# Bank ring left to the fill products, w_out scaled off GpSimd, ones of v written once, and new engine lists

## Chip, cores and metric

One core of one Trainium2 chip runs the whole program. The metric is the device time of one execution in microseconds; the kernel before takes 240.79 us (median of 3 runs, 240.64 to 241.34). Engines: TensorE (PE; PEld is its weight load), VectorE (DVE), ScalarE (ACT), GpSimd (POOL) and SyncE (SP), whose queue issues nearly all transfers.

## What is computed

```python
# q, k, v: (8 batches, 8 heads, 576 rows, 64); p: (8, 8, 32, 64); all float32
def sm_attn(qq, kk, vv):                       # softmax attention, scale 1/8
    s = scale * np.matmul(qq, kk.transpose(0, 1, 3, 2))
    a = np.exp(s - np.max(s, axis=-1, keepdims=True))
    a = a / (np.sum(a, axis=-1, keepdims=True) + 1e-09)
    return np.matmul(a, vv)
p_packed = sm_attn(p, k, v)                    # 32 packed rows per head
out = sm_attn(q, p_packed, p_packed)
x = out.transpose(0, 2, 1, 3).reshape(4608, 512)
h = x @ w_in                                   # 512 x 2048
g = h * (1.0 / (1.0 + np.exp(-beta * h)))
return g @ w_out                               # 2048 x 512, float32
```

## The kernel before

Eight batches of 576 rows go through three stages that overlap: attention over the packed rows, the first layer (`h`, then `g` on ScalarE), the second layer (`o` or `p`/`P` products into the output). The second softmax is folded into the first layer: `W = pp x w_in`, scaled by `beta` (L944), replaces x @ w_in, and `A2` holds the normalised weights. `w_out` is divided by `beta` row by row when it is cast to bf16 (`cast_out`, L1466).

- The order of work is written out by hand. `SEQUENCE` (L86) holds one list of task keys for each of PE, ACT, DVE, POOL and SP. A planner (`Planner.run`, L305) walks the lists with a cost for each task and emits the instructions; on the chip each engine runs its list in order, and an instruction that waits holds up everything behind it on its engine.
- A task key names its kind and batch: `("h", b, ft)` is one 128-column block of the first layer (two matmuls of 512 columns, 0.43 us), `("g", b, ft)` its activation; `("o", 0, t, ft)` one pair of second-layer matmuls of batch 0; `("p"/"P", b, i, ...)` the seven half-size products that stand for eight in batches 1 to 7, which need sums of `w_out` quarters (`("T4", i)`, L1133, all sixteen `w_out` blocks first) and sums of `g` (`("S", b, i)`); `("w", b, n)` and `("W", b, m)` the fused weights on PE and their scaling on DVE; `("s1", b, i)`, `("pun", b)`, `("s2", b, i)`, `("z2", b, i)` the attention products; `("hr", b, half)` the remaining 64 rows of a batch; `("take"/"add", 0, t)` reads of an output bank.
- Batches 0 and 1 are transposed on PE (`tr`, `trr`), batches 2 to 7 by transfers (`("tr", b, "k" or "q", 0)` on SP, L597). Each input has one float32 buffer, so the load of batch b waits for the casts of batch b - 1; the casts of batches 2 to 7 all run on POOL (`piece`, L506; `tail`, L520). For v, `piece` also writes the column of ones that counts the softmax sum (L511), once in each batch.
- The weights come through three staging buffers: `ld_in` 0, 1, `ld_out` 0, 1, `ld_in` 2, 3, `ld_out` 2, the rest of p, `ld_out` 3. Each waits for the casts of the load three places before it (`put_in` and `put_out`, L1471 and L1476). A `w_in` load is cast in two tasks `("w_in", n, i)`, a `w_out` load in four `("w_out", 4n + i)`.
- PSUM has eight banks in three rings: "h" (2), "o" (2), "att" (4). `HOME` (L63) puts single attention tasks of the start into a ring other than their own. Where a list leaves PE idle by the planner's costs in the first 60 us, `fill` (L344) lets `keep_warm` (L440) emit 128-column products on `ones`, but only while a bank of ring "o" is free; these products go into that bank.

Of the kernel before, what the change touches and what calls it, by code (L numbers as in the profile page):

```python
# [48 lines left out]
PE_BATCHES = 2  # L49
def TILED(key):  # L50
# [19 lines left out]
    ("s1", 0, 1): "h",  # L70
    ("z1", 0): "o",
    ("s2", 0, 1): "h",
    ("z2", 0, 0): "o",
    ("z2", 0, 1): "o",
    ("z2", 0, 2): "o",
# [1476 lines left out]
```

## Time and profile before

| | us |
|---|---|
| median of 3 runs | 240.79 |
| the profiled execution | 241.07 |
| its span, first to last instruction | 239.3 |
| PE busy in the span | 224.5 (94%) |
| ACT busy | 171.3 (72%) |
| DVE busy | 160.9 (67%) |
| POOL busy | 82.5 (34%) |
| mean granted TensorE clock | 0.986 of full speed |
| transfers, queue of SP | 53.75 MB, 81.5% of 16 engines' span |

The profiled execution lies 1.8 us above its span (start and end of the program) and 0.3 us above the median. PE has the largest share of busy time, but the share is a mean over a start that waits for data and a long stretch without gaps, so the stages are looked at one by one.

### The profile page before, as it was taken

The page shows a single profiled execution, that of the slowest core. Times are in us where ns is not written, and L with a number is a line of the kernel's source. Part 1 is how long each engine was busy: PE and PEld are TensorE (multiplying, and loading weights), DVE is VectorE, ACT ScalarE, POOL GpSimd, SP SyncE. Part 2 cuts the span into 40 slices and gives each one's busy share as a digit, 9 for nine tenths or more (in the row PEclk, how much of TensorE's full clock was granted, in tenths as well). Part 3 has the DMA queues.
Part 4 walks back from the last instruction along what each step waited for, and adds up shares of the span by engine and source line. Part 5 has one row for each costly group of instructions (what it writes and reads, how often), then busy time and mean ns, then how long its engine had stood idle before and what let it go on. Part 6 is the DMA issues. An engine that isn't in the chain of part 4 may idle for free.

```text
span 239.3 us, 6112 instructions
## 1 busy us (share of the span) xinstructions
PE 224.5 (94%) x2550; PEld 152.9 (64%) x2576; DVE 160.9 (67%) x254; ACT 171.3 (72%) x312; POOL 82.5 (34%) x90
## 2 busy tenths in 40 slices
PE   7887899986999999999999999999999999999993
PEld 6554353333477765775588567876786578677883
DVE  4569647884897945986798855852788279515751
ACT  3619679874899977977679678896788679665300
POOL 3223448398873160624151730540354000000000
PEclk9999589999999999999999999999999999999999
DMA  6999999999999999999999899969794040022044
GB/s 216 396 387 399 401 350 348 290 325 224 263 263 191 274 275 245 218 320 242 230 279 331 225 236 303 225 128 221 160 313 147 3 175 3 1 86 92 0 122 144
DMA packets 67107, 54.14 MB, mean 226 GB/s; under 512 B 38948, under 2 KB 58532, under 8 KB 66568
## 3 DMA queue, kind: packets, MB, share of 16 engines
q1 hardware_dynamic: 67072, 53.75, 81.5%
q8 instruction: 20, 0.33, 0.6%
q14 instruction: 7, 0.06, 0.1%
q10 hardware_dynamic: 8, 0.01, 0.0%
HBM read 37.23 MB, written 9.44 MB: 195 GB/s over the span
## 4 chain that ended last, share of the span: by engine, by line
PE 72%; DMA 11%; POOL 5%; ACT 4%; DVE 3%; issue 2%; SPq 1%; POOLq 0%; DVEq 0%
PE o_ps L421 42%; PE h_ps L421 19%; DMA k<-in_k_dram 6%; DMA w_in<-in_moe_w_in_dram 5%; POOL w_out_bf L1469 3%; PE w_ps L421 3%; PE hr_ps L421 3%; PE s_ps L421 2%; PE pp_ps L421 1%; PE z_ps L421 1%; ACT g_main L992 1%; POOL k_bf L515 1%; DVE g_main L1223 1%; DVE W_bf L957 1%; ACT L438 1%
## 5 line engine op out<-in xcount | busy, mean ns | idle before, releaser
L992 ACT ACTIVATE g_main<-h_ps 128x512 bf16<-128x512 f32 x128 | 72.2, 596 | 34.9 <-PE h_ps L421 28.1
L421 PEld LDWEIGHTS <-g_main 128*128 128x128 bf16 x624 | 58.8, 98 | 25.8 <-issue 5.3
L421 PE MATMUL h_ps<-A2T,W_bf 128*128 128x512 bf16 x233 | 68.5, 390 | 1.8 <-DVE A2T L890 1.0
L421 PE MATMUL o_ps<-w_out_bf,g_main 128*128 128x256 bf16 (+1 forms) x397 | 61.2, 289 | 2.3 <-POOL w_out_bf L1469 1.9
L421 PEld LDWEIGHTS <-W_bf 128*128 128x128 bf16 x512 | 33.2, 99 | 20.6 <-issue 6.6
L950 DVE TENSOR_TENSOR W_bf<-w_ps,beta_bc 128x512 bf16<-128x512 f32 x48 | 30.6, 684 | 15.8 <-PE w_ps L421 15.8
L421 PE MATMUL o_ps<-w_sum,g_sum 128*128 128x256 bf16 x256 | 33.1, 273 | 0.6 <-DVE o_sb L1253 0.4
L421 PE MATMUL o_ps<-w_sum,g_main 128*128 128x256 bf16 x224 | 31.3, 273 | 0.3
L1253 DVE TENSOR_TENSOR o_sb<-o_ps,o_sb 128x512 f32<-128x512 f32 (+1 forms) x27 | 17.0, 630 | 18.9 <-PE o_ps L421 15.6
L438 ACT ACT_TABLE_LOAD x22 | 28.2, 1283 | 1.1 <-PEq L1536 0.7
L421 PEld LDWEIGHTS <-g_sum 128*128 128x128 bf16 x256 | 24.3, 98 | 6.3 <-issue 1.0
L515 POOL CAST q_bf<-q 128x1024 bf16<-128x1024 f32 x12 | 13.6, 1151 | 31.2 <-DMA q<-in_q_dram 31.2
L515 POOL CAST v_bf<-v 128x1024 bf16<-128x1024 f32 x12 | 15.6, 1326 | 22.4 <-DMA v<-in_v_dram 22.4
L1255 ACT COPY o_sb<-o_ps 128x512 f32<-128x512 f32 (+1 forms) x16 | 8.1, 506 | 14.1 <-PE o_ps L421 14.1
L515 POOL CAST k_bf<-k 128x1024 bf16<-128x1024 f32 x12 | 13.3, 1124 | 12.8 <-DMA k<-in_k_dram 12.8
L1255 DVE COPY o_sb<-o_ps 128x512 f32<-128x512 f32 (+1 forms) x20 | 13.2, 661 | 4.1 <-PE o_ps L421 4.0
L957 DVE SCALAR_TENSOR_TENSOR W_bf<-w_ps,rz,beta_bc 128x512 bf16<-128x512 f32 x15 | 10.4, 745 | 4.2 <-PE w_ps L421 4.2
L890 DVE TENSOR_TENSOR A2T<-E2T,rz 128x512 bf16<-128x512 bf16 x16 | 11.6, 733 | 2.1 <-ACT rz L885 1.8
L1469 POOL TENSOR_SCALAR w_out_bf<-w_out,rbeta 128x512 bf16<-128x512 f32 x6 | 10.6, 1768 | 4.8 <-DMA w_out<-in_moe_w_out_dram 4.7
L1223 DVE TENSOR_TENSOR g_sum<-g_main 128x2048 bf16<-128x2048 bf16 x7 | 9.0, 1283 | 3.9 <-ACT g_main L992 3.9
L421 PE MATMUL w_ps<-w_in_bf,pp 64*32 64x512 bf16 x252 | 11.1, 389 | 0.0
L873 ACT ACTIVATE rz<-z_ps 128x512 f32<-128x512 f32 x16 | 9.6, 604 | 1.9 <-PE z_ps L421 1.9
(131 smaller groups left out, 281.3 us busy)
## 6 DMA issues: line engine op xcount, KB each, us to landing
k<-in_k_dram SPq DMA_DIRECT2D x6, 1024.0 KB, 8.7
v<-in_v_dram SPq DMA_DIRECT2D x6, 1024.0 KB, 8.3
q<-in_q_dram SPq DMA_DIRECT2D x6, 1024.0 KB, 9.2
out_dram<-o_sb SPq DMA_DIRECT2D x10, 512.0 KB, 3.7
w_in<-in_moe_w_in_dram SPq DMA_DIRECT2D x4, 1024.0 KB, 11.5
w_out<-in_moe_w_out_dram SPq DMA_DIRECT2D x4, 1024.0 KB, 10.7
out_dram<-o_sb SPq DMA_DIRECT2D x12, 256.0 KB, 3.8
k<-in_k_dram SPq DMA_DIRECT2D x4, 576.0 KB, 6.4
```

The lines of the kernel that those rows point to most:

```text
L421: return self.nc.tensor.matmul(out, lhsT, rhs, start=start, stop=stop, tile_position=pos, skip_group_check=True)
L438: self.nc.scalar.preload_act_table_set(SETS[mode])
L515: self.copy[engine](o[:, 0 : 32 * e].rearrange("p (t h e) -> p h t e", t=4, h=8)[:, h, :, 0:D], t[:, 0:2048].rearrange("p (h t d) -> p h t ...
L873: nc.scalar.activation(st[b, "rz2"][:, i], ps[:], AF.Ln)
L890: nc.vector.tensor_tensor(part(st[b, "A2"], i), part(st[b, "E2"], i), st[b, "rz2"][:, i] if i < 2 else st[b, "rz2r"][:], ALU.mult)
L950: nc.vector.tensor_tensor(st[b, "W"][:, r, cols].rearrange("q (f p) -> q f p", f=4), st[b, "w", m][:].rearrange("q (p f) -> q f p", f=4), ...
L957: nc.vector.scalar_tensor_tensor(st[b, "W"][:, r, cols].rearrange("q (f p) -> q f p", f=4), st[b, "w", m][:].rearrange("q (p f) -> q f p", ...
L992: nc.scalar.activation(st[b, "g"][:, ft, :], st[b, "h", ft][:], AF.Silu)
L1223: nc.vector.tensor_tensor(o, x, y, op)
L1253: nc.vector.tensor_tensor(o, x, o, ALU.add)
L1255: self.copy[engine](o, x)
L1469: nc.scalar.mul(o, w, r) if engine == "ACT" else {"DVE": nc.vector, "POOL": nc.gpsimd}[engine].tensor_scalar_mul(o, w, r)
```

## The change

Four things are changed.

1. `HOME`: no attention task of the start goes into ring "o" any more; `p0_tr`, `trr 0 k`, `s1r 0`, `z2 0 2`, `w 0 0`, `tr 1 k 0` go to "h", `bcol` and `brow` 0 to 3 to "att", `tr 1 q 0` stays in "att". Ring "o" is then free until the first second-layer product.
2. `cast_out` has no GpSimd form: POOL's six `w_out` blocks (4, 6, 8, 10, 12, 15) go to DVE, but for 12, which goes to ACT (ACT gives 7 and 14 to DVE and takes 1). DVE scales 13 of the 16 blocks, before 7.
3. The ones of v are written once, in the first batch cast by `piece`; the later batches use the same tile.
4. All five lists are in a new order. On DVE, `w_in` blocks (1, 0), before, become (1, 1), (2, 0), (3, 0), and `p_bf` comes from POOL. POOL takes casts of batches 0 and 1 from ACT. SP loads k of batch 0 ahead of p0, v of batch 1 ahead of `ld_out` 0, k of batch 2 ahead of `ld_in` 3, and q of batch 2 ahead of `ld_out` 3 and of v of batch 2.

```diff
 HOME = {
-    ("brow", 0): "o",
-    ("brow", 2): "o",
+    ("p0_tr",): "h",
+    ("bcol",): "att",
+    ("brow", 0): "att",
...
-    ("s1r", 0): "o",
+    ("s1r", 0): "h",
...
-    ("w", 0, 0): "o",
-    ("tr", 1, "k", 0): "o",
+    ("z2", 0, 2): "h",
+    ("w", 0, 0): "h",
+    ("tr", 1, "k", 0): "h",
...
-    ("tr", 1, "q", 0): "o",
...
     "PE": [
-        ("z2", 0, 0), ("brow", 3), ("s2", 0, 1), ("z2", 0, 1), ("s1r", 1), ("s1", 1, 1), ("w", 0, 0), ("s1", 1, 0),
-        ("z2", 0, 2), ("h", 0, 1), ("h", 0, 0), ("w", 0, 1), ("z1", 1), ("h", 0, 2), ("h", 0, 3), ("tr", 1, "q", 0),
...
+        ("z2", 0, 0), ("tr", 1, "k", 1), ("trr", 1, "k"), ("z2", 0, 1), ("s2", 0, 1), ("s1r", 1), ("s1", 1, 0),
+        ("w", 0, 0), ("s1", 1, 1), ("w", 0, 1), ("z2", 0, 2), ("z1", 1), ("h", 0, 3), ("h", 0, 1), ("pun", 1, 0),
+        ("pun", 1), ("h", 0, 0), ("h", 0, 2), ("tr", 1, "q", 0), ("h", 0, 5), ("h", 0, 4), ("tr", 1, "q", 1),
+        ("h", 0, 6), ("h", 0, 7), ("w", 1, 0), ("o", 0, 0, 1), ("o", 0, 2, 1), ("o", 0, 2, 3), ("trr", 1, "q"),
+        ("s2", 1, 0), ("o", 0, 0, 3), ("o", 0, 0, 5), ("o", 0, 2, 5), ("z2", 1, 0), ("o", 0, 0, 7), ("o", 0, 2, 7),
+        ("z2", 1, 1), ("w", 0, 2), ("w", 1, 1), ("s2", 1, 1), ("o", 0, 3, 1), ("o", 0, 3, 3), ("w", 1, 2),
...
+        ("o", 0, 0, 13), ("h", 1, 14), ("h", 1, 8), ("o", 0, 2, 9), ("h", 1, 12), ("o", 0, 2, 11), ("s1r", 2),
+        ("hr", 0, 0), ("h", 1, 15), ("o", 0, 0, 15), ("o", 0, 2, 13), ("s1", 2, 1), ("s1", 2, 0), ("o", 0, 2, 15),
+        ("o", 0, 3, 9), ("o", 0, 3, 11), ("hr", 0, 1), ("o", 0, 3, 13), ("o", 0, 3, 15), ("p", 1, 1, 0),
...
     "DVE": [
...
-        ("i1", 0), ("px", 0), ("T", 1, "k", 0), ("pn", 0), ("beta", 2), ("T", 1, "k", 1), ("rk", 1), ("w_in", 0, 1),
-        ("A2", 0, 0), ("w_in", 1, 0), ("W", 0, 0), ("W", 0, 1), ("A2", 0, 1), ("W", 0, 2), ("W", 0, 3), ("w_out", 0),
-        ("w_out", 1), ("i1", 1), ("w_out", 2), ("T", 1, "q", 0), ("T", 1, "q", 1), ("pp", 1), ("px", 1), ("w_out", 5),
...
+        ("pp", 0), ("rq", 0), ("px", 0), ("T", 1, "k", 0), ("beta", 3), ("T", 1, "k", 1), ("w_in", 0, 1), ("rk", 1),
+        ("A2", 0, 0), ("W", 0, 0), ("w_in", 1, 1), ("W", 0, 1), ("A2", 0, 1), ("W", 0, 2), ("W", 0, 3),
+        ("cast", 1, "q", 0), ("pp", 1), ("i1", 1), ("T", 1, "q", 0), ("px", 1), ("w_out", 0), ("w_out", 2),
+        ("T", 1, "q", 1), ("W", 1, 0), ("w_out", 5), ("w_out", 4), ("w_out", 6), ("w_out", 7), ("W", 1, 1),
+        ("w_in", 2, 0), ("rq", 1), ("take", 0, 0), ("W", 0, 4), ("W", 0, 5), ("take", 0, 2), ("W", 1, 2),
+        ("A2", 0, 2), ("W", 1, 3), ("A2", 1, 0), ("A2", 1, 1), ("W", 1, 4), ("w_in", 3, 0), ("W", 1, 5), ("p_bf",),
+        ("W", 0, 6), ("W", 0, 7), ("take", 0, 3), ("w_out", 9), ("w_out", 8), ("w_out", 11), ("take", 0, 1),
+        ("W", 1, 6), ("w_out", 10), ("W", 1, 7), ("pT1", 0, 1), ("pT1", 1, 0), ("w_out", 13), ("w_out", 14),
+        ("w_out", 15), ("T4", 1), ("add", 0, 1), ("T4", 2), ("T4", 3), ("T4", 4), ("add", 0, 0), ("S", 1, 1),
...
     "POOL": [
-        ("cast", 1, "q", 0), ("cast", 1, "q", 1), ("cast", 1, "v", 1), ("w_out", 4), ("pn", 1), ("w_out", 6),
-        ("w_in", 2, 1), ("w_in", 3, 1), ("w_in", 3, 0), ("cast", 2, "k", 0), ("w_out", 8), ("cast", 2, "k", 1),
-        ("cast", 2, "k", 2), ("p_bf",), ("w_out", 10), ("w_out", 15), ("w_out", 12), ("cast", 2, "v", 0),
...
+        ("w_in", 0, 0), ("pn", 0), ("w_in", 1, 0), ("cast", 1, "v", 0), ("cast", 1, "v", 1), ("cast", 1, "q", 1),
+        ("pn", 1), ("cast", 2, "k", 0), ("cast", 2, "k", 1), ("w_in", 3, 1), ("cast", 2, "k", 2), ("cast", 2, "q", 0),
...
     "SP": [
...
+        ("ld", 0, "v", 1), ("ld", 1, "k", 0), ("ld", 1, "k", 1), ("ld_in", 0), ("ld_in", 1), ("ld", 1, "v", 0),
+        ("ld", 1, "v", 1), ("ld", 1, "q", 0), ("ld", 1, "q", 1), ("ld_out", 0), ("ld_out", 1), ("ld_in", 2),
+        ("ld", 2, "k", 0), ("ld_in", 3), ("ld", 2, "k", 2), ("ld", "p"), ("ld_out", 2), ("ld", 2, "q", 0),
+        ("ld_out", 3), ("ld", 2, "q", 2), ("tr", 2, "k", 0), ("ld", 2, "v", 0), ("ld", 2, "v", 2), ("ld", 3, "k", 0),
...
-                if i == 0:
+                if i == 0 and x == "v" and b > PE_BATCHES:
+                    self.t[b, x] = self.t[b - 1, x]
+                elif i == 0:
...
-            nc.scalar.mul(o, w, r) if engine == "ACT" else {"DVE": nc.vector, "POOL": nc.gpsimd}[engine].tensor_scalar_mul(o, w, r)
+            nc.vector.tensor_scalar_mul(o, w, r) if engine == "DVE" else nc.scalar.mul(o, w, r)
```

## Rows read from the trace of the kernel before

**Rows 1.** Page, busy tenths, granted clock and transfers in 40 slices of 5.98 us.

```profile
PE   7887899986999999999999999999999999999993
PEclk9999589999999999999999999999999999999999
DMA  6999999999999999999999899969794040022044
```

**Rows 2.** Stages: us, PE PEld DVE ACT POOL busy (count), clock, transfer share, GB/s.

```profile
25.00:30.00 5.00, 4.79 (x33) 2.13 (x33) 2.88 (x6) 3.29 (x6) 2.30 (x2) 0.50 1.06 403
30.00:35.00 5.00, 4.95 (x67) 2.96 (x66) 1.92 (x5) 3.64 (x6) 2.44 (x2) 0.86 0.93 347
80.00:100.00 20.00, 19.72 (x239) 13.02 (x240) 14.00 (x19) 16.06 (x31) 8.85 (x10) 1.00 1.11 252
```

**Rows 3.** PE in order of time: start, us, work [idle before <-releaser], to 57 us.

```profile
23.96 0.23 PE L421 MATMUL z2r_ps<-E2T,bones 128*128 128x128 bf16 x1 [1.18 <-DVE W_bf L957]
25.21 1.44 PE L421 MATMUL h_ps<-A2T,W_bf 128*128 128x512 bf16 x3 [1.02 <-DVE A2T L890]
...
56.94 0.59 PE L421 MATMUL o_ps<-w_out_bf,g_main 128*128 128x512 bf16 x2 [1.90 <-POOL w_out_bf L1469]
57.37 0.59 PE L421 MATMUL h_ps<-A2T,W_bf 128*128 128x512 bf16 x2
```

**Rows 4.** DVE in order of time: a cast, a pair of neighbours, the last T4.

```profile
22.55 0.69 DVE L1458 CAST w_in_bf<-w_in 128x1024 bf16<-128x1024 f32 x1 [0.47 <-DMA w_in<-in_moe_w_in_dram]
...
39.22 0.68 DVE L1054 COPY o_sb<-o_ps 128x512 f32<-128x512 f32 x1
39.82 1.41 DVE L957 SCALAR_TENSOR_TENSOR W_bf<-w_ps,rz,beta_bc 128x512 bf16<-128x512 f32 x2
...
64.39 1.38 DVE L1133 TENSOR_TENSOR w_sum<-w_out_bf,w_sum 128x2048 bf16<-128x2048 bf16 x1
```

**Rows 5.** Weight tiles: durations in ns min/median/max, and issue to landing.

```profile
L1469 DVE TENSOR_SCALAR w_out_bf<-w_out,rbeta x7: 471/656/925, 28.6 to 51.2; 128x512 bf16<-128x512 f32 x7
L1469 POOL TENSOR_SCALAR w_out_bf<-w_out,rbeta x6: 1557/1567/2625, 33.7 to 55.3; 128x512 bf16<-128x512 f32 x6
DMA to landing us min/median/max: 8.7/10.7/15.1
...
L1458 DVE CAST w_in_bf<-w_in x2: 694/1016/1337, 20.1 to 22.6; 128x1024 bf16<-128x1024 f32 x2
```

**Rows 6.** DVE groups from 36 to 66 us: count | busy, mean ns.

```profile
L957 DVE SCALAR_TENSOR_TENSOR W_bf<-w_ps,rz,beta_bc 128x512 bf16<-128x512 f32 x12 | 8.3, 745 | 2.1 <-PE w_ps L421 2.1
L1133 DVE TENSOR_TENSOR w_sum<-w_out_bf 128x2048 bf16<-128x2048 bf16 x2 | 3.3, 1639 | 0.6 <-POOL w_out_bf L1469 0.6
L1133 DVE TENSOR_TENSOR w_sum<-w_out_bf,w_sum 128x2048 bf16<-128x2048 bf16 x2 | 2.8, 1376 | 0.0
```

**Rows 7.** POOL in order of time: weights, ones, v of batch 3.

```profile
33.71 1.57 POOL L1469 TENSOR_SCALAR w_out_bf<-w_out,rbeta 128x512 bf16<-128x512 f32 x1 [1.38 <-DMA w_out<-in_moe_w_out_dram]
...
51.02 5.87 POOL L1469 TENSOR_SCALAR w_out_bf<-w_out,rbeta 128x512 bf16<-128x512 f32 x3
56.84 0.25 POOL L511 MEMSET v_bf<- 128x36 bf16 x1
...
83.13 2.02 POOL L515 CAST v_bf<-v 128x1024 bf16<-128x1024 f32 x2 [8.23 <-DMA v<-in_v_dram]
85.10 0.46 POOL L522 CAST v_bf<-v 128x256 bf16<-128x256 f32 x1
```

**Rows 8.** SP's queue in order of time: `ld_out` 3.

```profile
41.17 0.35 SPq L1462 DMA_DIRECT2D w_out<-in_moe_w_out_dram  x1
```

**Rows 9.** PE in order of time: first product of batch 1, pun of batch 3.

```profile
66.75 0.63 PE L421 MATMUL hr_ps<-A2T,W_bf 128*128 128x64 bf16 x16
67.22 0.60 PE L421 MATMUL o_ps<-w_out_bf,g_main 128*128 128x256 bf16 x4
...
87.33 0.49 PE L421 MATMUL pp_ps<-v_bf,E1T 128*32 128x65 bf16 x40
```

More of the change, by code (lines that the diff above doesn't have):

```diff
@@ L63 @@
 HOME = {
-    ("brow", 0): "o",
-    ("brow", 2): "o",
+    ("p0_tr",): "h",
+    ("bcol",): "att",
+    ("brow", 0): "att",
+    ("brow", 1): "att",
+    ("brow", 2): "att",
     ("brow", 3): "att",
+    ("trr", 0, "k"): "h",
     ("tr", 0, "q", 1): "h",
-    ("s1r", 0): "o",
+    ("s1r", 0): "h",
     ("s1", 0, 0): "h",
[L70 to L75, printed above, removed]
-    ("w", 0, 0): "o",
-    ("tr", 1, "k", 0): "o",
+    ("z2", 0, 2): "h",
+    ("w", 0, 0): "h",
+    ("tr", 1, "k", 0): "h",
     ("tr", 1, "k", 1): "h",
-    ("tr", 1, "q", 0): "o",
     ("s1", 1, 1): "h",
     ("s2", 1, 0): "h",
+    ("s2", 1, 1): "h",
     ("z2", 1, 0): "h",
@@ L87 @@
     "PE": [
[75 rows of a table removed]
[75 rows of a table added]
     ],
     "ACT": [
[37 rows of a table removed]
[36 rows of a table added]
     ],
     "DVE": [
[7 rows of a table removed]
-        ("W", 1, 6), ("W", 1, 7), ("w_out", 9), ("take", 0, 3), ("w_out", 11), ("w_out", 13), ("T4", 1),
[22 rows of a table removed]
[8 rows of a table added]
+        ("W", 0, 6), ("W", 0, 7), ("take", 0, 3), ("w_out", 9), ("w_out", 8), ("w_out", 11), ("take", 0, 1),
[24 rows of a table added]
     ],
     "POOL": [
-        ("cast", 0, "q", 0), ("cast", 0, "v", 0), ("cast", 1, "k", 0), ("w_in", 0, 0), ("w_in", 1, 1),
-        ("cast", 1, "q", 0), ("cast", 1, "q", 1), ("cast", 1, "v", 1), ("w_out", 4), ("pn", 1), ("w_out", 6),
-        ("w_in", 2, 1), ("w_in", 3, 1), ("w_in", 3, 0), ("cast", 2, "k", 0), ("w_out", 8), ("cast", 2, "k", 1),
-        ("cast", 2, "k", 2), ("p_bf",), ("w_out", 10), ("w_out", 15), ("w_out", 12), ("cast", 2, "v", 0),
[1 row of a table removed]
+        ("cast", 0, "k", 1), ("cast", 0, "q", 0), ("cast", 0, "v", 0), ("cast", 1, "k", 0), ("cast", 1, "k", 1),
+        ("w_in", 0, 0), ("pn", 0), ("w_in", 1, 0), ("cast", 1, "v", 0), ("cast", 1, "v", 1), ("cast", 1, "q", 1),
[2 rows of a table added]
         ("cast", 3, "k", 0), ("cast", 3, "k", 2), ("cast", 3, "k", 1), ("cast", 3, "q", 0), ("cast", 3, "q", 1),
@@ L245 @@
         ("cast", 5, "k", 2), ("cast", 5, "v", 0), ("cast", 5, "v", 1), ("cast", 5, "v", 2), ("cast", 6, "k", 0),
[4 rows of a table removed]
[4 rows of a table added]
     ],
     "SP": [
[14 rows of a table removed]
-        ("store", 12), ("store", 11), ("store", 14), ("store", 13), ("store", 16, 0), ("store", "r1", 0),
-        ("store", "r1", 1), ("store", 17, 1), ("store", 16, 1), ("store", 17, 0),
[14 rows of a table added]
+        ("store", 11), ("store", 14), ("store", 13), ("store", "r1", 0), ("store", "r1", 1), ("store", 16, 0),
+        ("store", 17, 1), ("store", 16, 1), ("store", 17, 0),
     ],
@@ L540, in plan_loads @@
             else:
-                c0 = self.task(("cast", b, x, 0), "POOL", 0.97, lambda f=piece: f("POOL", 0, 4), [m0] + old, rank + 3)
+                c0 = self.task(("cast", b, x, 0), "POOL", 1.35 if b == PE_BATCHES and x == "v" else 0.97, lambda f=piece: f("POOL", 0, 4), [m0] + old, rank + 3)
                 self.task(("cast", b, x, 1), "POOL", 0.97, lambda f=piece: f("POOL", 1, 4), [m0, c0], rank + 3)
@@ L1479, in put_out @@
                 [
-                    self.task(("w_out", 4 * n + i), {"DVE": 0.4, "ACT": 0.7, "POOL": 0.8}, None, lambda e, i=i: cast_out(e, n, i), [ld, ("rbeta",)], rank)
+                    self.task(("w_out", 4 * n + i), {"DVE": 0.45, "ACT": 0.7}, None, lambda e, i=i: cast_out(e, n, i), [ld, ("rbeta",)], rank)
                     for i in range(4)
```

296 rows, old and new, of the table SEQUENCE are left out of this document.

## The prediction

> **What bounds the kernel now.** I read the slices of the page first, then the stages, then each engine in order of time. The slices show PE at nine tenths or more from slice 10 to the last but one, at full clock, and weaker before 66 us [rows 1]. The stage from 80 to 100 us has 19.72 us of PE in 20.00 [rows 2]: no other engine can give much there, and PE in order ends the run. What a change of lists is worth is therefore how much sooner PE comes to that packed stretch, unless inputs are late afterwards. Three losses stand before it. PE waits 1.18 and then 1.02 us for DVE ahead of the first h product at 25.21 [rows 3]. After that gap the granted clock is 0.50 from 25 to 30 us (1.2 instead of 2.4 GHz) and 0.86 from 30 to 35 [rows 2]: 4.79 x 0.50 + 4.95 x 0.14 = 3.1 us of PE time. At 56.94 PE has waited 1.90 us for a `w_out` block on POOL, which scaled three in 5.87 us [rows 3, 7]. The transfer engines stand at eight tenths or more from slice 1 to slice 25 [rows 1], so a load comes earlier only if another comes later.
>
> **Ring "o" and the fill products.** Before, "o" was taken by attention tasks in the gap ahead of 25.21, so nothing could fill it. With "o" free, the gap can be filled and the clock should stay at 2.4 GHz: 3.1 us of PE time come back. Whether they reach the end depends on what PE waits for next, below.
>
> **Start of h.** On DVE, W(0,0) stood behind the cast of `w_in`(1,0), which waited for its load until 22.55 [rows 4]. Now W(0,0) is ahead, and after the load come one cast, W(0,1) and A2. The cast costs 0.69 to 1.34 [rows 5]; before, one cast, two W and A2 stood there. That saves one W (0.745 less 0.08 overlap [rows 4, 6]) if the cast takes 0.69, nothing if it takes 1.34: 0 to 0.7 us, I take 0.3. k ahead of p0 at the front gains at most one issue, about 0.35 [rows 8]; not counted.
>
> **w_out off POOL.** POOL loses six blocks of 1.557 to 2.625 us, DVE gains six of 0.471 to 0.925 (mean 0.656) [rows 5], two casts of `w_in` more, and p. This removes the wait of 1.90, but it lays the weights into one DVE queue with W, the bank reads and T4, so I add that queue up. The load of `w_out` 4 to 7 lands at 33.7, where POOL had waited for it [rows 7], and the same set of loads stands ahead of it afterwards. From there DVE has four blocks and W(1,1): with 0.08 us of overlap between neighbours (39.22 + 0.68 against 39.82 [rows 4]) 4 x 0.58 + 0.66, so `w_in`(2,0) starts at 36.7. From it to the end of T4(4) the new list holds 10 W of 0.665, 7 `w_out` of 0.576, 2 `w_in` of 0.94, four T4 (3.3 + 2.8 less 0.3 = 5.8), four bank takes and one add of 0.60 each (pitch [rows 4]), and two full and one small A2, rq, p and two pT1, which I estimate at 3.4 together from the same rows. That is 6.65 + 4.0 + 1.9 + 5.8 + 3.0 + 3.4 = 24.75, hence 61.4. In this stretch W waited 2.1 us for its PSUM [rows 6]; I allow a third, 0.7, so 62.1. Before, T4(4) ended at 64.39 + 1.38 = 65.8.
>
> **SP's queue.** `ld_out` 3 now waits for `w_in`(3,0) on DVE and stands behind the megabyte of q of batch 2. In the list above that cast ends 8.0 us after 36.7; with part of the waits the issue is at 45.2, against 41.17 before [rows 8]. Behind it on SP wait the rest of q, the k transpose of batch 2, v of batch 2 and k of batch 3. Its landing is not known: the four `w_out` loads took 8.7 to 15.1 us, median 10.7 [rows 5]. Before, the load issued at 41.17 had a block scaled on DVE at 51.2 [rows 5], so it took under 10.1. I take 9.3, near that one: 54.5. DVE comes to `w_out` 13 at 54.0 (62.1 less 5.8, 0.6 and three blocks), so 0.5 more is waited and T4(4) ends at 62.6.
>
> **What PE does with it.** o(0,3,9) needs the bank that add(0,0) frees, right behind T4(4): 63.2. Four pairs at 0.43 (56.94 to 57.37 [rows 3]) and one hr of 0.47 (66.75 to 67.22 [rows 9]) follow, and p(1,1,0) starts at 65.4. Before it started at 67.22 [rows 9], with 0.9 us of products (one hr, one pair) still to come that now lie ahead. Gain: 67.2 + 0.9 - 65.4 = 2.7 us. PE itself would be there no later: the 3.1 of clock, the 1.90 and the 0.3 make 5.3, so about 2.6 of it goes into new waits for DVE and loads.
>
> **What is late next.** pun of batch 3 ran at 87.33; its v was cast by 85.10 + 0.46 = 85.56 after POOL had waited 8.23 us for the load [rows 7, 9]. The new list has one h block more ahead (0.43), so PE wants it at 87.33 + 0.43 - 2.7 = 85.1: 0.5 too early if v comes as before. Transfers are full and the same loads stand ahead of v, so I give back 0.1 to 0.5, and take 0.1 because other weights no longer hold POOL. Net 2.6.
>
> **Ones of v.** Five memsets of 0.25 us leave POOL [rows 7]: 1.3 us, hidden behind its waits for loads (8.23 at 83.13); worth nothing, at most 1.3 if POOL were the bound. ACT keeps three `w_out` blocks and loses four casts of batches 0 and 1; it waits for loads there, so nothing.
>
> **A rule against it.** DVE's blocks spread from 0.471 to 0.925 and its casts from 0.694 to 1.337 while POOL was casting [rows 5]. The Trainium skill, SBUF — State Buffer, "Who interferes with whom", says that DVE and GpSimd share one port pair as an exclusive lock: a cast or tensor_scalar in a two-port mode, or a tensor_tensor with two SBUF inputs, that comes second waits for the whole GpSimd instruction. By it seven blocks and two casts could each lose a whole POOL cast (2.02 for two [rows 7]), 9 x 1.0 = 9 us, and the kernel would be slower; an estimate from that page and this row. The rows show at most 0.45 over the fastest, so I go by them.
>
> **Rivals.**
> (A) PE is given all back: DVE runs at its fast end (7 x 0.19 + 2 x 0.32 = 1.9 less) without the 0.7 and 0.5 of waits, T4(4) ends at 59.5, and PE's own 5.3 decide: 240.8 - 5.3 = 235.5. For it: PE's losses are there in the rows. Against: it wants over thirty instructions in a row on DVE without a wait, beside POOL's casts.
> (B) No change: DVE at its slow end, 7 x (0.925 - 0.656) + 2 x (1.337 - 1.016) = 2.5 us, eats the gain: 240.7. Or the change doesn't do what it says: fill products are emitted only for planned idle time, the gap comes where none was planned, the clock falls as before, and of its 3.1 some 1.2 lies under the new waits: 2.6 - 1.9, or 240.1. For it: 7 to 13 blocks on DVE beside POOL's casts. Against: POOL itself has less to do there.
> (C) Slower: `ld_out` 3 lands late. T4 stands behind it on DVE, add(0,0) behind T4, and PE behind that; every us past 54.5 is a us at the end. The gain is gone at 57.1, 11.9 us after the issue; at 15.1 after the issue it lands at 60.3 and the time is 240.8 - 2.6 + 5.8 = 244.0; halfway, 242.4. For it: the issue itself is 4 us later, a megabyte more is ahead of it, and the median of the four is 10.7. Against: the two loads nearest in place took 8.7 and under 10.1.
>
> **Numbers.** Profiled execution 241.07, that is 0.3 over the median; the forecast stands against the median: 240.8 - 2.6 = 238.2. Chances: forecast 0.56 (its own range 236.6 to 239.8), A 0.16, B 0.15, C 0.13. Some 0.02 of B falls among the faster and 0.02 of C among the unchanged, so faster by over 0.3% (0.7 us, what a measurement of this kernel can tell from none) 0.74, within 0.3% 0.15, slower 0.11. The range takes in B, most of A and the near part of C: 235.4 to 241.3.
>
> **What would show it.** Clock: granted 1.00 from 25 to 35 us; if it is 0.5 anywhere there, the ring did nothing. DVE: T4(4) ending near 62.6, `w_out` blocks near 0.6; ends near 65 speak for B. SP: `ld_out` 3 issued near 45, first of its blocks on DVE near 54.5; past 57 is C. PE: p(1,1,0) near 65.4, and no idle over 1 us before pun of batch 3. The forecast is wrong if PE waits for loads after 70 us, where it has not waited before.

## Result and profile after

The changed kernel takes 239.69 us (median of 20 runs, 237.28 to 244.03), the kernel before beside it 241.36 (240.39 to 242.65): a ratio of 0.991, 95% interval 0.989 to 0.993. Two later comparisons gave 0.987 (0.984 to 0.990) and 0.988 (0.984 to 0.992). So it is faster by 0.9 to 1.3%, 2 to 3 us. The ratios leave out executions that took over 1.5% more than the fastest of the same kernel: six of these twenty (241.48 to 244.03 us) and none of before, so that the medians of all, 239.69 and 241.36, give only 0.993. The profiled execution took 238.5 us where that of before took 241.07: 2.6 us less. Its span is 236.4.

The slices of the page, as in [rows 1]:

```profile
PE   7799999999999899899999999999999999999993
PEclk9999999999999999999999999999999999999999
DMA  6999999999998999999999998999974322021313
```

The stages, as in [rows 2] (length, busy PE, PEld, DVE, ACT, POOL, then clock, transfer share, GB/s):

```profile
25.00:30.00 5.00, 4.80 (x89) 3.27 (x90) 4.82 (x10) 4.07 (x7) 3.11 (x3) 1.00 1.05 417
30.00:35.00 5.00, 5.00 (x43) 2.37 (x43) 4.42 (x11) 4.78 (x8) 0.46 (x2) 1.00 1.01 380
...
80.00:100.00 20.00, 18.82 (x239) 12.34 (x239) 14.54 (x22) 15.53 (x32) 5.14 (x7) 1.00 1.09 226
```

The half-clock of 25 to 35 us is gone. But 80 to 100 us, PE's packed stretch, has 0.9 us less of PE busy. PE in order of time, as in [rows 3, 9]:

```profile
20.54 1.79 PE L421 MATMUL o_ps<-ones 128*128 128x128 bf16 x29
...
23.04 1.29 PE L421 MATMUL o_ps<-ones 128*128 128x128 bf16 x20
...
25.99 0.66 PE L421 MATMUL o_ps<-ones 128*128 128x128 bf16 x9
26.49 0.81 PE L421 MATMUL h_ps<-A2T,W_bf 128*128 128x512 bf16 x3
...
54.67 0.59 PE L421 MATMUL o_ps<-w_out_bf,g_main 128*128 128x512 bf16 x2 [0.52 <-ACT w_out_bf L1471]
...
61.42 1.46 PE L421 MATMUL o_ps<-w_out_bf,g_main 128*128 128x512 bf16 x6
...
63.18 1.46 PE L421 MATMUL o_ps<-w_out_bf,g_main 128*128 128x512 bf16 x8
...
68.87 0.41 PE L421 MATMUL s_ps<-qT,pp 64*32 64x512 bf16 x8 [0.58 <-DMA qT<-q_bf]
...
99.28 0.29 PE L421 MATMUL s1r_ps<-pT,kT 128*128 128x128 bf16 x2 [1.07 <-DMA kT<-k_bf]
```

Fills stand where PE waited, and h starts at 26.49, later than before: the row at 25.21 [rows 3] is the second h matmul there, since the record of the first is missing (its weights were loaded at 23.97). The wait of 1.90 us ahead of phase B (the products that need the last `w_out` blocks) is 0.52. The row at 63.18 holds two pairs and then the four half products of p(1,1,0), which therefore start at 63.18 + 4 x 0.216 = 64.05; before it was 67.22, with 0.9 us of products still to come that now lie ahead. The last two rows are new: PE waits for transfers after 66 us.

DVE in order of time, as in [rows 4, 6]:

```profile
23.17 0.75 DVE L959 SCALAR_TENSOR_TENSOR W_bf<-w_ps,rz,beta_bc 128x512 bf16<-128x512 f32 x1 [1.12 <-PE w_ps L421]
...
33.62 1.67 DVE L1471 TENSOR_SCALAR w_out_bf<-w_out,rbeta 128x512 bf16<-128x512 f32 x4 [0.26 <-DMA w_out<-in_moe_w_out_dram]
...
36.35 0.69 DVE L1460 CAST w_in_bf<-w_in 128x1024 bf16<-128x1024 f32 x1 [0.40 <-DMA w_in<-in_moe_w_in_dram]
...
53.90 1.42 DVE L1471 TENSOR_SCALAR w_out_bf<-w_out,rbeta 128x512 bf16<-128x512 f32 x3 [1.04 <-DMA w_out<-in_moe_w_out_dram]
...
59.36 1.22 DVE L1135 TENSOR_TENSOR w_sum<-w_out_bf,w_sum 128x2048 bf16<-128x2048 bf16 x1
60.72 0.69 DVE L1060 TENSOR_TENSOR o_sb<-o_ps,o_sb 128x512 f32<-128x512 f32 x1
```

The tile row of the scaled blocks (ns min/median/max), as in [rows 5]:

```profile
L1471 DVE TENSOR_SCALAR w_out_bf<-w_out,rbeta x13: 473/479/619, 31.1 to 54.7; 128x512 bf16<-128x512 f32 x13
```

SP's queue, `ld_out` 3, as in [rows 8]:

```profile
44.92 0.33 SPq L1464 DMA_DIRECT2D w_out<-in_moe_w_out_dram  x1
```

T4(4) ends at 59.36 + 1.22 = 60.6 (before 65.8), the row behind it is add(0,0), and a block takes 0.48 us in the median (before 0.66 on DVE, 1.57 on POOL [rows 5]).

To compare kernels along the run I use PE's lead: how much earlier than the kernel before PE had done the same share of its useful products (fills left out, each shape at its median pitch). It is worked out from the matmul rows of both traces. Some records are missing, so it is good to some tenths, in a few places to 0.8 only. All runs below are in one table; the ratio is to the kernel before on the same chip.

| kernel | median us | ratio (95%) | lead at 36 us | 52 | 60 | 100 | 220 |
|---|---|---|---|---|---|---|---|
| changed, first trace | 239.69 | 0.991 (0.989 to 0.993) | 2.3 | 2.4 | 3.9 | 3.0 | 2.9 |
| e1 changed again | 238.40 | 0.987 (0.984 to 0.990) | 1.9 | 2.2 | 3.8 | 3.6 | 3.5 |
| e2 fills to 20 us | 238.98 | 0.989 (0.986 to 0.991) | 4.0 | 2.6 | 3.9 | 3.0 | 2.5 |
| e3 six blocks on POOL | 240.81 | 0.997 (0.994 to 0.999) | -1.5 | -1.7 | 0.0 | -0.3 | -0.4 |
| e4 ones each batch | 238.84 | 0.988 (0.986 to 0.991) | | | | | |
| e5 before, ring alone | 242.03 | 1.003 (1.000 to 1.006) | -2.9 | -2.6 | -2.6 | -2.3 | -1.4 |
| e6 before, `w_out` alone | 238.98 | 0.990 (0.985 to 0.994) | -0.5 | 0.5 | 2.5 | 2.5 | 2.0 |
| e7 transfer of k first | 238.11 | 0.987 (0.983 to 0.992) | 2.1 | 2.3 | 4.0 | 4.0 | 3.5 |
| e8 fills to 12 us | 237.00 | 0.983 (0.978 to 0.988) | 2.0 | 2.5 | 4.0 | 4.8 | 5.1 |
| e9 changed, third | 238.68 | 0.988 (0.984 to 0.992) | 2.2 | 1.9 | 3.2 | 3.0 | 3.1 |
| e10 e8 and e7 | 237.57 | 0.983 (0.979 to 0.988) | 3.4 | 2.5 | 4.0 | 4.5 | 3.6 |
| e11 `ld_out` 3 first | 238.24 | 0.986 (0.982 to 0.990) | 1.8 | 2.4 | 4.6 | 3.5 | 3.8 |
| e12 two blocks on POOL | 241.54 | 1.001 (0.998 to 1.004) | 2.1 | 1.8 | 0.4 | 1.1 | 1.1 |

The lead is made in two steps: about 2 us by 36 us, and about 2 at 53 to 55 us, where the kernel before stood in its wait of 1.90.

### The profile page after: what moved, and what is told of

Same layout as the page of the kernel before. It is cut to its first block, busy times and chain, and to the rows that moved or that the text cites. A ratio compares the mean times of both kernels' runs of the same rounds, so it can differ in the third digit from the quotient of the medians.

```text
span 236.4 us, 6257 instructions
## 1 busy us (share of the span) xinstructions
PE 225.2 (95%) x2626; PEld 156.8 (66%) x2651; DVE 166.0 (70%) x269; ACT 167.4 (71%) x302; POOL 66.1 (28%) x80
## 4 chain that ended last, share of the span: by engine, by line
PE 71%; DMA 21%; DVE 2%; SPq 2%; issue 1%; ACT 1%; POOL 1%; POOLq 0%
PE o_ps L421 40%; PE h_ps L421 16%; DMA q<-in_q_dram 6%; DMA w_in<-in_moe_w_in_dram 5%; DMA kT<-k_bf 4%; DMA qT<-q_bf 4%; DMA k<-in_k_dram 3%; PE w_ps L421 3%; PE hr_ps L421 2%; PE s_ps L421 2%; PE brow_ps L421 2%; PE pp_ps L421 1%; PE z_ps L421 1%; POOL q_bf L517 1%; SPq L485 1%
## 5 line engine op out<-in xcount | busy, mean ns | idle before, releaser
L421 PE MATMUL h_ps<-A2T,W_bf 128*128 128x512 bf16 x232 | 66.1, 379 | 0.5
L421 PE MATMUL o_ps<-w_out_bf,g_main 128*128 128x256 bf16 (+1 forms) x399 | 60.7, 289 | 1.4 <-DVE o_sb L1257 0.6
L421 PE MATMUL o_ps<-w_sum,g_sum 128*128 128x256 bf16 x256 | 33.4, 273 | 0.2
L517 POOL CAST v_bf<-v 128x1024 bf16<-128x1024 f32 x12 | 13.5, 1156 | 38.4 <-DMA v<-in_v_dram 25.2
L1257 DVE COPY o_sb<-o_ps 128x512 f32<-128x512 f32 (+1 forms) x26 | 16.0, 615 | 11.5 <-PE o_ps L421 10.4
L517 POOL CAST q_bf<-q 128x1024 bf16<-128x1024 f32 x12 | 12.8, 1078 | 25.2 <-DMA q<-in_q_dram 23.6
L517 POOL CAST k_bf<-k 128x1024 bf16<-128x1024 f32 x12 | 12.5, 1064 | 21.3 <-DMA k<-in_k_dram 19.8
L1257 ACT COPY o_sb<-o_ps 128x512 f32<-128x512 f32 (+1 forms) x10 | 5.6, 565 | 13.7 <-PE o_ps L421 13.6
L421 PE MATMUL o_ps<-ones 128*128 128x128 bf16 x159 | 13.7, 241 | 1.1 <-DVE ones L1304 1.1
L892 DVE TENSOR_TENSOR A2T<-E2T,rz 128x512 bf16<-128x512 bf16 x16 | 12.6, 794 | 0.7 <-ACT rz L887 0.7
L421 PEld LDWEIGHTS <-ones 128*128 128x128 bf16 x159 | 11.3, 110 | 2.6 <-DVE ones L1304 1.1
L959 DVE SCALAR_TENSOR_TENSOR W_bf<-w_ps,rz,beta_bc 128x512 bf16<-128x512 f32 x16 | 11.6, 742 | 1.2 <-PE w_ps L421 1.1
```

What stands on the lines that cost most here:

```text
L421: return self.nc.tensor.matmul(out, lhsT, rhs, start=start, stop=stop, tile_position=pos, skip_group_check=True)
L517: self.copy[engine](o[:, 0 : 32 * e].rearrange("p (t h e) -> p h t e", t=4, h=8)[:, h, :, 0:D], t[:, 0:2048].rearrange("p (h t d) -> p h t ...
L892: nc.vector.tensor_tensor(part(st[b, "A2"], i), part(st[b, "E2"], i), st[b, "rz2"][:, i] if i < 2 else st[b, "rz2r"][:], ALU.mult)
L959: nc.vector.scalar_tensor_tensor(st[b, "W"][:, r, cols].rearrange("q (f p) -> q f p", f=4), st[b, "w", m][:].rearrange("q (p f) -> q f p", ...
L1257: self.copy[engine](o, x)
```

## Experiments

My theory: the two last `w_out` blocks on POOL set the start of phase B, and moving them is the gain; fills and clock change when the early work is done, not the end. Rivals: the clock is the gain; or the transfers are.

### The same kernel again (e1, e9)

> The changed kernel unchanged, timed beside the kernel before on the chip that the next three share. Its first runs gave 0.991 of before (0.989 to 0.993) and spread over 237.3 to 244.0 us where before spread over 240.4 to 242.7. If what was measured belongs to the kernel, the ratio comes out at 0.988 to 0.994 again, the clock of 25 to 35 us reads 1.00, h starts at about 26.5 us, the first scale of batch 1 (p 1 1 0) at about 64.1 us, and the wait for kT 4 at 99 us (1.07 us) stands again. If the chip made it (a chip on which transfers are slower), ratio and waits behind 68 us come out otherwise while the part up to 64 us stays.

> The changed kernel unchanged, as the row beside which the next three are read on the same chip. Two comparisons so far gave 0.991 (0.989 to 0.993) and 0.987 (0.984 to 0.990) of before; a third between 0.985 and 0.993 is expected by every theory.

The ratios were 0.987 and 0.988, the clock 1.00 from 15 us on in both. h started at 27.1 and 26.6 us, p(1,1,0) at 64.15 and 64.70, and the wait for kT 4 took 0.42 and 0.40 us in place of 1.07. So the first 64 us repeat to within 0.7 us, and the later waits vary by about as much from one execution to the next.

### Fills to 20 us (e2)

```diff
-WARM_UNTIL = 60.0
+WARM_UNTIL = 20.0
```

> Changed kernel with WARM_UNTIL 20 us in place of 60 us: no fill product behind the ones at about 20 us. Theory (the fills hold the clock, the clock is worth some 3 us of PE up to 35 us, of which the chain on DVE hides a part): the granted clock of 25 to 30 us falls to 0.5 to 0.8 again, h starts near 25 us in place of 26.5, w_out blocks 4 to 7 wait for their transfer all the same, T4(4) ends within 0.5 us of where it ends with fills (60.6 us), and the loss at the end is 0.5 to 2 us against the changed kernel. Rival 1 (the clock is what the change is worth): T4(4) and p 1 1 0 come 2.5 to 3 us later, and the whole gain over before is gone. Rival 2 (the fills only hold up s1r 1 and h, by 1.5 us): the clock falls little or not, p 1 1 0 comes up to 1 us earlier, and the kernel is 0.5 to 1 us faster.

Stage rows of this kernel:

```profile
20.00:25.00 5.00, 3.93 (x89) 2.70 (x87) 4.41 (x8) 3.67 (x10) 4.10 (x5) 1.00 1.06 389
25.00:30.00 5.00, 4.11 (x60) 2.25 (x61) 4.44 (x11) 4.50 (x8) 2.76 (x5) 1.00 1.04 418
```

Its PE in order of time:

```profile
24.85 0.38 PE L421 MATMUL h_ps<-A2T,W_bf 128*128 128x512 bf16 x1
...
25.70 0.59 PE L421 MATMUL h_ps<-A2T,W_bf 128*128 128x512 bf16 x2 [0.47 <-DVE A2T L892]
```

Its DVE:

```profile
33.42 1.68 DVE L1471 TENSOR_SCALAR w_out_bf<-w_out,rbeta 128x512 bf16<-128x512 f32 x4 [0.30 <-DMA w_out<-in_moe_w_out_dram]
...
36.16 0.69 DVE L1460 CAST w_in_bf<-w_in 128x1024 bf16<-128x1024 f32 x1 [0.40 <-DMA w_in<-in_moe_w_in_dram]
```

The clock did not fall, against my theory and rival 1: it held without the fills behind 20 us. The first h matmul came at 24.85, 1.6 us earlier than in the first trace, the next at 25.70, and PE led by 4.0 us at 36 us in place of 2.3, since fills that outlast the wait which they cover hold PE up. At 52 us all of that was gone: DVE waits for the loads of `w_out` and `w_in` at 33.4 and 36.2 just the same, and T4(4) ended at 60.8. The median lies 0.6 us above e1, and the six runs of each overlap: no difference that was measured.

### Fills to 12 us (e8)

```diff
-WARM_UNTIL = 60.0
+WARM_UNTIL = 12.0
```

> Changed kernel with fills only up to 12 us of the planned time (the run with a limit of 20 us kept the clock at 1.00 and lost 0.6 us, within its interval). Theory A (the fills of 15 to 20 us, 25 of them, bring the clock up and PE's own work holds it from there): the clock of some stretch between 15 and 30 us falls to 0.5, PE does its work of 15 to 35 us 1 to 3 us later, and since VectorE waits for the w_out 12 to 15 transfer at 54 us all the same, the end moves by less than 0.7 us. Theory B (the order of the new lists alone keeps PE dense enough): the clock stays at 1.00 and the time is that of the run with 20 us. Rival (the lead up to 35 us does carry to the end): the time is 1.5 us or more above the changed kernel.

Stage rows of this kernel:

```profile
20.00:25.00 5.00, 3.00 (x52) 1.52 (x53) 3.90 (x7) 2.56 (x7) 4.13 (x5) 0.72 1.06 389
25.00:30.00 5.00, 4.89 (x64) 2.67 (x64) 4.04 (x8) 3.40 (x7) 2.88 (x3) 0.60 1.04 417
```

Its PE in order of time:

```profile
25.46 1.92 PE L421 MATMUL h_ps<-A2T,W_bf 128*128 128x512 bf16 x4
...
54.68 0.59 PE L421 MATMUL o_ps<-w_out_bf,g_main 128*128 128x512 bf16 x2 [0.40 <-ACT w_out_bf L1471]
```

With 58 fills in place of 159 the half-clock is back (the first four h matmuls take 1.92 us), and it costs nothing: the lead at 36 and 52 us is that of the changed kernel, phase B starts at 54.68 against 54.67, and the median is not longer but 1.1 us shorter than that of e7, the nearest kernel on the same chip, with runs that overlap. Theory A had the clock right; whether the time moved by more than its 0.7 us, and downwards, these runs do not show. The rival (1.5 us or more above the changed kernel) fell.

### The ring alone (e5)

Only the places in `HOME` of the kernel before (`z1` 0 and `z2` 0 0 and 0 1 go to att likewise, `z2` 0 2 to h; `brow` 0 goes to h here, to att in the change):

```diff
-    ("brow", 0): "o",
-    ("brow", 2): "o",
+    ("brow", 0): "h",
+    ("brow", 2): "att",
...
-    ("s1r", 0): "o",
+    ("s1r", 0): "h",
...
-    ("w", 0, 0): "o",
-    ("tr", 1, "k", 0): "o",
+    ("w", 0, 0): "h",
+    ("tr", 1, "k", 0): "h",
...
-    ("tr", 1, "q", 0): "o",
+    ("tr", 1, "q", 0): "att",
```

> Kernel before with its lists as they were, and nothing changed but that the ten small products that stood in the output ring (brow 0 and 2, s1r 0, z1 0, z2 0, w 0 0, tr 1 k 0, tr 1 q 0) stand in the rings att and h, so that fills may run between them. That is part one of the change by itself. Theory (the ring and its fills pay nothing at the end, since blocks 12 and 15 of w_out from GpSimd set the start of phase B): more fills between 15 and 30 us than the 9 of before, granted clock near 1.00 from 25 to 35 us, PE's useful work 1 to 3 us ahead at 36 us, the wait at 57 us for GpSimd's block grows from 1.90 to 3 or 4 us, and the time is that of before within 0.8 us. Rival 1 (the clock is what the change is worth): 2 to 3 us faster. Rival 2 (the small products crowd att and h): the lead is not made and the time is 0.5 to 2 us longer.

A stage row of this kernel:

```profile
25.00:30.00 5.00, 5.00 (x110) 4.44 (x108) 2.64 (x5) 3.23 (x9) 2.29 (x2) 1.00 1.07 400
```

Its PE in order of time:

```profile
25.81 2.35 PE L421 MATMUL o_ps<-ones 128*128 128x128 bf16 x39
...
30.88 1.03 PE L421 MATMUL h_ps<-A2T,W_bf 128*128 128x512 bf16 x4
...
59.47 0.59 PE L421 MATMUL o_ps<-w_out_bf,g_main 128*128 128x512 bf16 x2 [1.25 <-POOL w_out_bf L1469]
```

The clock is full, but PE is 7.6 us behind at 30 us, not ahead as my theory had it: rival 2's crowded rings, and 233 fills. The wait for POOL shrank to 1.25 us where it was to grow to 3 or 4. Yet the time is only 0.3% longer (0 to 0.6), so of the 5.7 us that h lost (30.88 against 25.21) little reached the end. The ring by itself gains nothing. How much of the loss is rings and how much fills stays open.

### `w_out` alone (e6)

The kernel before, its lists and ring kept; 4, 6, 8, 10, 14, 15 on DVE and 12 on ACT:

```diff
 "DVE": [ ...
-        ("w_out", 9), ("take", 0, 3), ("w_out", 11), ("w_out", 13), ("T4", 1),
+        ("w_out", 9), ("w_out", 8), ("take", 0, 3), ("w_out", 11), ("w_out", 10), ("w_out", 13), ("w_out", 14), ("w_out", 15), ("T4", 1),
```

> Kernel before with GpSimd's six blocks of w_out moved to VectorE (4, 6, 8, 10, 14, 15) and ScalarE (12 in place of 14): part two of the change by itself, on the old lists and with the old ring. Theory (the block from GpSimd was the wait ahead of phase B): the wait of 1.90 us at 57 us is gone, the half-clock stays (0.5 at 25 to 30 us), T4(4) ends 2 to 3 us ahead of 65.8 us, and the time is 1.5 to 2.5 us shorter. Rival (the six blocks are 3.5 us more on VectorE, which is the next bound, or PE's late start is): the time moves by less than 0.5 us.

A stage row of this kernel:

```profile
25.00:30.00 5.00, 3.51 (x26) 1.34 (x27) 3.64 (x7) 3.81 (x7) 2.43 (x2) 0.78 1.07 404
```

Its PE, the row of p(1,1,0):

```profile
64.73 0.60 PE L421 MATMUL o_ps<-w_out_bf,g_main 128*128 128x256 bf16 x4
```

The wait of 1.90 is gone, p(1,1,0) starts at 64.73 in place of 67.22, and the ratio is 0.990: the gain of the whole change, within the intervals, on the old lists. Two expectations missed: the granted clock is 0.78 from 25 to 30 us, not 0.5, and T4(4) ends at 61.90 + 2.02 = 63.9, 1.9 us ahead of before and not 2 to 3. The lead is still -0.5 us at 36 us, so the gain owes nothing to the start.

### Blocks back on POOL (e3, e12)

e3 puts all six blocks back on POOL, e12 only the last two:

```diff
 "POOL": [ ...
-        ("cast", 2, "q", 0), ("cast", 2, "q", 1), ("cast", 2, "q", 2),
+        ("cast", 2, "q", 0), ("cast", 2, "q", 1), ("w_out", 15), ("w_out", 12), ("cast", 2, "q", 2),
```

> Changed kernel with the six blocks of w_out that it took from GpSimd (4, 6, 8, 10, 12, 15) back there, at the places among its casts that they had before; the other lists stay. Theory (the scaling of w_out on GpSimd set the start of phase B): blocks 12 and 15 come 2 to 4 us later than w_out 13 to 15 of the changed kernel (53.9 us), PE waits 1.5 to 3 us ahead of the o products that use them, T4(4) and p 1 1 0 come 2 to 3 us later, and the time is 1.5 to 3 us longer, most of the gain over before. Rival (PE's clock and its work set the start of phase B, or the transfer of w_out 12 to 15 does, and POOL was only the last to be seen): p 1 1 0 moves by under 0.7 us and the time by under 0.5 us.

> Changed kernel with only two blocks of w_out back on GpSimd, 15 and 12, behind its cast of the second part of q of batch 2; blocks 4, 6, 8 and 10 stay on VectorE. With all six back the loss was 2.4 us, and the lead over before was lost in two places: 4 us at 34 us, and the wait of 1.42 us at 58.8 us. Theory (the last two blocks are the price that phase B pays, as the wait of 1.90 us in the kernel before says): the blocks come out 1.5 to 3 us after 54.7 us, PE waits 1 to 2.5 us more there, and the time is 1 to 2 us longer. Rival (blocks 4 and 6 are the price, since PE's first o products wait for them at 31 to 36 us, and the later wait only shows slack that was lost before): PE waits at 55 us but the end moves by less than 0.5 us.

PE of e3 in order of time:

```profile
31.75 3.46 PE L421 MATMUL o_ps<-ones 128*128 128x128 bf16 x59
...
58.75 0.59 PE L421 MATMUL o_ps<-w_out_bf,g_main 128*128 128x512 bf16 x2 [1.42 <-POOL w_out_bf L1471]
```

POOL of e3:

```profile
33.51 1.57 POOL L1471 TENSOR_SCALAR w_out_bf<-w_out,rbeta 128x512 bf16<-128x512 f32 x1 [3.84 <-DMA w_out<-in_moe_w_out_dram]
35.14 0.52 POOL L779 COPY pp<-px 64x64 bf16<-64x64 bf16 x2
```

PE of e12:

```profile
58.49 0.59 PE L421 MATMUL o_ps<-w_out_bf,g_main 128*128 128x512 bf16 x2 [3.52 <-POOL w_out_bf L1471]
```

POOL of e12:

```profile
54.63 3.81 POOL L1471 TENSOR_SCALAR w_out_bf<-w_out,rbeta 128x512 bf16<-128x512 f32 x2 [0.92 <-DMA w_out<-in_moe_w_out_dram]
```

The tile row of POOL's blocks in e12:

```profile
L1471 POOL TENSOR_SCALAR w_out_bf<-w_out,rbeta x2: 1850/1914/1978, 54.6 to 56.5; 128x512 bf16<-128x512 f32 x2
```

Six blocks back cost 2.4 us against e1, as the theory had it, though p(1,1,0) came at 68.99, 4.8 us later than in e1 and not 2 to 3. Two blocks are enough to lose all: 1.001, 2.9 us above the changed kernel on the same chip, more than the 1 to 2 expected. (That two cost more than six lies within the intervals, 0.994 to 0.999 against 0.998 to 1.004.) The load lands at 54.5, POOL takes 1.9 us a block, and PE stands for 3.52 us. That is the price of phase B, and the rival (blocks 4 and 6 alone) fell. Block 4 has a price of its own in e3: POOL waits 3.84 us for its load, the copy for pn 1 stands behind it to 35.14, and PE's next work with it. PE shows no idle there, since 59 fills stand in the gap at 31.75: a fill counts as busy, so such a wait is read from what PE did.

### The landing of `ld_out` 3 (e11)

```diff
-        ("ld", 2, "q", 0), ("ld_out", 3), ("ld", 2, "q", 2),
+        ("ld_out", 3), ("ld", 2, "q", 0), ("ld", 2, "q", 2),
```

> Changed kernel with the load of w_out blocks 12 to 15 ahead of the first load of q of batch 2 on SyncE's queue (both 1 MB). In the changed kernel it is issued at 45.3 us, VectorE and ScalarE wait 0.9 and 0.7 us for it and PE 0.4 us at 54.8 us, after which PE has no gap to 66 us. Theory (the landing of this load is now what comes last ahead of phase B, with little behind it): it lands 2 to 4 us earlier, the three waits go, T4(4) ends about 0.9 us earlier and p 1 1 0 0.3 to 0.6 us earlier, the time is 0 to 0.6 us shorter. Rival 1 (VectorE's list sets phase B): p 1 1 0 comes 0.9 us earlier or more and so does the end. Rival 2 (q of batch 2 takes its place): q lands about 3 us later, s2 2 waits 1 us or more in place of 0.6, and the time is 0.5 to 2 us longer.

DVE of this kernel:

```profile
52.97 1.26 DVE L1471 TENSOR_SCALAR w_out_bf<-w_out,rbeta 128x512 bf16<-128x512 f32 x3
54.15 1.21 DVE L1135 TENSOR_TENSOR w_sum<-w_out_bf 128x2048 bf16<-128x2048 bf16 x1
...
56.32 2.01 DVE L1135 TENSOR_TENSOR w_sum<-w_out_bf,w_sum 128x2048 bf16<-128x2048 bf16 x1
...
59.59 1.21 DVE L1135 TENSOR_TENSOR w_sum<-w_out_bf,w_sum 128x2048 bf16<-128x2048 bf16 x1
```

Its POOL:

```profile
53.95 3.30 POOL L517 CAST q_bf<-q 128x1024 bf16<-128x1024 f32 x2 [8.49 <-PE h_ps L421]
```

Its PE:

```profile
60.90 1.57 PE L421 MATMUL o_ps<-w_out_bf,g_main 128*128 128x512 bf16 x6
...
62.78 1.47 PE L421 MATMUL o_ps<-w_out_bf,g_main 128*128 128x512 bf16 x8
...
68.79 0.41 PE L421 MATMUL s_ps<-qT,pp 64*32 64x512 bf16 x8 [0.90 <-DMA qT<-q_bf]
```

The waits for this load are gone, and p(1,1,0) starts at 62.78 + 0.87 = 63.65 against 64.15 and 64.70 in e1 and e9. T4(4) ends at 60.8, no earlier than in e1 (60.7; e9 61.2): POOL's casts of q now fall beside it, and one T4 takes 2.01 us. Against e1, whose first 52 us are alike, PE moved without T4(4), so T4 is not what sets phase B in the changed kernel. It stands close behind: there PE comes to o(0,3,9) at 61.42 + 2 x 0.216 = 61.85, 0.4 us after add(0,0) has freed the bank (60.72 + 0.69 = 61.41). Here PE is there first and stands for 0.1 us (six matmuls take 1.57 us in place of 1.46), so T4(4) and add(0,0) are the next bound. The wait for qT grew to 0.90, and the time is 0.4 us below e9, within the runs' scatter.

### What is behind 66 us (e7, e4, e10)

e7 moves the transfer of k of batch 4 ahead of a store, e10 does that with fills to 12 us, e4 writes the ones of every batch.

```diff
-        ("store", 2), ("tr", 4, "k", 0),
+        ("tr", 4, "k", 0), ("store", 2),
```

> Changed kernel with one pair on SyncE's queue swapped: the transposing transfer of k of batch 4 is issued ahead of the stores of output block 2. Theory (part of the lead was given back to transfers that SyncE issues late): s1r 4 waits for kT 4 0.4 to 1.1 us at 99 us in the changed kernel; the stores hold the queue 1.27 us; the wait goes, and the time is 0.3 to 0.9 us shorter. Rival (those waits take nothing, because what follows waits for ScalarE or VectorE anyway, or the store frees late the block that the next output is written into): within 0.3 us.

> Changed kernel with the ones column of v written for every batch again, as before. Theory (POOL is idle a good part of the time and the ones are no one's wait): 0 within 0.3 us; the small POOL instructions are there again behind 85 us and nothing waits for them. Rival (they push the casts of v of batch 3 and on, and so pun 3): at most 0.1 us a batch, 0.5 us in all.

> Changed kernel with fills only up to 12 us of the planned time and with the transposing transfer of k of batch 4 ahead of the stores of output block 2: the two edits that gave the lowest times so far (0.983 and 0.987 of before, on one chip). Theory (fills behind 12 us buy nothing at the end although the clock is 0.6 to 0.7 from 20 to 30 us without them; the late transfer costs little): the time is that of the changed kernel or up to 1.5 us below, ratio to before 0.980 to 0.989, and the half-clock is there again. Rival 1 (the fills pay, and the run without them was a lucky draw): 0.5 us or more above the changed kernel of this call. Rival 2 (the fills themselves cost, since they hold PE when its inputs are ready): at least 1 us below the changed kernel of this call, outside both intervals.

In e7 the wait for kT 4 is gone and the lead at 100 us is 4.0, but at 220 us it is 3.5 as in e1, and the ratio too is that of e1 (on another chip; the changed kernel was not run beside e7): the rival held. e4 lies 0.4 us above e1, inside their scatter: the ones are worth nothing. e10, with a clock of 0.84 and 0.82 from 20 to 30 us, is 1.1 us below e9, as e8 was 1.1 below e7. Both times the ratio of the medians is 0.995, and both times the runs overlap. Few fills are thus likely the better version, and the lowest time of the study (237.0 us); no trace names its cause.

## Why the prediction held, and where it did not

The forecast was 238.2, a gain of 2.6 us; the profiled execution gained 2.6, the three comparisons 1.7 to 3.2. The size was right, but that it fits to a tenth is luck: two terms in the sum were mis-sized, with opposite signs.

Two stages of the kernel before that the steps below need, 30 to 66 and 70 to 130 us:

```profile
30.00:66.00 36.00, 32.93 (x256) 14.55 (x258) 25.97 (x41) 27.92 (x47) 25.84 (x24) 0.98 1.08 299
...
70.00:130.00 60.00, 59.12 (x741) 41.77 (x744) 46.39 (x66) 48.61 (x93) 21.55 (x26) 1.00 1.06 261
```

The same of the changed kernel; the fifth engine is POOL:

```profile
30.00:66.00 36.00, 34.59 (x307) 16.79 (x310) 32.85 (x54) 30.98 (x55) 11.94 (x15) 1.00 1.10 303
...
70.00:130.00 60.00, 57.87 (x748) 40.65 (x753) 44.60 (x67) 48.44 (x90) 19.60 (x23) 1.00 1.06 252
```

- **Clock and ring.** 1.00 from 25 to 35 us, as forecast. That its 3.1 us would mostly go into new waits is shown: with the half-clock back (e8) phase B starts at the same time, and the ring alone (e5) gains nothing.
- **Start of h.** Forecast 0.3 us earlier, measured at least 1.3 later: I filled the gap with fills and did not ask whether they outlast it. Nor did W(0,0) gain by its place ahead of the cast of `w_in`(1,0): DVE waited 1.12 us for its product from PE and started it at 23.17, as before (23.16); in e2 it waited 0.59 us. The late h cost nothing at the end, because the DVE list hangs on the landing of the loads at 33.6 and 36.4 us, as the step on `w_out` 4 to 7 said (33.7 and 36.7).
- **DVE list.** This step failed in size. T4(4) ended at 60.6, not 62.6. Seven blocks took 1.26 + 0.47 + 1.42 - 0.2 = 2.9 us, not 4.0, and four T4 4 x 1.13 = 4.5, not 5.8: 2.4 us less. What was saved ahead of `ld_out` 3 went into the wait of 1.04 us for it; of the 2.0 us by which T4(4) came early, 0.6 are the load's earlier landing and 1.4 the shorter work behind it. I had taken durations from [rows 5, 6], where POOL worked beside DVE, and the change itself takes that work from POOL: between 30 and 66 us POOL is busy for 11.9 us, before 25.8. With that, T4(4) was no longer the bound that I named, by 0.4 us (e11). What sets phase B is the landing of `ld_out` 3 (issued 44.92, forecast 45.2; used at 53.90, forecast 54.5) and PE's own work behind it without a gap. p(1,1,0) came at 64.05, not 65.4: 1.3 us of gain too few.
- **What is late next.** I gave back 0.1 us, for v of batch 3; PE did not wait for it (pun at 84.99, forecast 85.1). Other waits came. PE's busy time from 70 to 130 us is 57.87 of 60 us against 59.12 before: 1.25 lost. The waits in it are 1.07 us for transposed k and 0.60 for a bank read, less one of 0.44 that before had; 0.58 for transposed q stands just ahead, at 68.87. My own sign that the forecast is wrong (PE waits for loads after 70 us) did appear, at 99 us; the 1.3 us above made up for it. Taking the wait for k away did not change the end (e7), so what takes the lead from 4.4 us at 66 us to 2.9 at 220 is not settled.
- **Rivals.** A (235.5) has its start on DVE, T4(4) at 60.6 against 59.5, but not its end, since a third of the lead made by then is gone at 220 us. B fell, since DVE ran at its fast end and the clock held. C did not come: the load landed 9.0 us after its issue. e12 shows that C's mechanism is real, with POOL in its place: phase B 3.2 us later than in e9 (58.49 against 55.32) is 2.9 at the end.
- **The sum.** I put the clock (3.1) beside the wait for POOL (1.90) as parts of what PE gets back. e6 shows that taking the blocks from POOL, with no gain in the start, brings as much as was measured. The first step of the lead, 2 us by 36 us, belongs to neither ring nor clock (e5, e8); the new order of the lists is left, which was not tried by itself, and little of this step can be seen in the times.

## What to carry to other kernels

Ask which piece is the last to arrive before the packed stretch, and move that piece from the slow engine: two blocks of 1.9 us were worth as much as the whole change. A stretch at half clock ahead of a load that lands late cost nothing here, and fills that keep the clock there can hold up real work and hide waits in the busy rows. When a change unloads an engine, take the durations of its neighbour from rows in which that engine was idle.
